# Applying the layer-norm weight vector where tokens are centred instead of in the weights, with weight loads spread over seven units and the next pair's loads gated

## The chip, the cores and the metric

One core of one Trainium2 chip. The metric is device time in microseconds (us) of one execution; lower is better. Every ratio below is to the kernel before, run in turn on the same chip. The runs came from several chips, so a difference of the medians of two runs is rougher than a difference of their ratios.

Engines are named as in the profile: PE is TensorE (matmuls), PEld its weight load, DVE is VectorE, ACT is ScalarE, POOL is GpSimd, SP is SyncE, which here only issues DMAs. The granted clock is the share of full speed that the profile shows for TensorE.

## The reference

Linear attention over 8 batches, 8 heads, 576 positions of 64; then, for each token of 512 numbers, a layer norm, two matmuls with a relu between, and a residual.

```python
def _attn_ref(q, k, v, w_phi):
    def phi(x):
        proj = np.einsum('bhsd,df->bhsf', x, w_phi)
        proj = proj - np.max(np.abs(proj), axis=-1, keepdims=True)
        return np.concatenate([np.exp(proj), np.exp(-proj)], axis=-1)
    ...
    return num / den

def _moe_ref(x, g_ln, w_ch1, w_ch2):
    mu = np.mean(x, axis=-1, keepdims=True)
    var = np.mean((x - mu) ** 2, axis=-1, keepdims=True)
    xn = (x - mu) / np.sqrt(var + 1e-06) * g_ln      # g_ln: 512 numbers
    ch = np.maximum(xn @ w_ch1, 0.0) @ w_ch2         # 512x2048, 2048x512
    return x + ch
```

The vector `g_ln` can be multiplied into the rows of `w_ch1` once (the kernel before) or into every centred token. The division by the standard deviation is done at the very end in both.

## The kernel before

The work is cut into 32 attention units, in four pairs of batches. When a pair's attention is done, its 9 tiles of 128 tokens go through the layer norm and the two matmuls in rounds of three tiles; a round has 16 evictions of the hidden layer (an eviction moves a matmul's result from its tile `hT_ps` to `hT`). While PE multiplies one pair, the other engines prepare the attention of the next. The kernel carries a small list scheduler: every operation is given a cost and a rank, and the kernel is emitted in the order that the scheduler finds. So a change of a cost or of a dependency can reorder all engines.

```python
    def load_w1(n, rank, after):                 # quarter n of w_ch1, 512 KB in bf16, GpSimd's DMA queue
        dma("POOL", rank, 1200000, w1_sb[:, :, n * WC : (n + 1) * WC], ...)

    def scale_w1(n, rank):                       # 4 scalings a chunk, 16 in all
        for kc in range(KC):
            def emit(e, kc=kc):
                w = w1_sb[:, kc, n * WC : (n + 1) * WC]
                ENG[e].tensor_scalar_mul(out=w, in0=w, scalar1=gln_sb[:, kc : kc + 1])
            add_any({"DVE": 0.22, "POOL": 0.62}, rank, emit, r=["gln"], w=[("w1", n, kc)])
    # ... (cut)
            def center(e, i=i, t=t):             # one tile of 128 tokens, on DVE or on POOL
                ENG[e].tensor_scalar(
                    out=pr["xc", r][:, i, :], in0=x[:, t, :],
                    scalar1=pr["mv"][:, t, 0:1], scalar2=None, op0=ALU.subtract,
                )
    # ... (cut)
    WEIGHTS = {0: (0,), 1: (1,), 2: (2,), 3: (3,), 4: (4,), 5: (5,), 6: (6,), 7: (7,)}
    # unit: chunks issued behind its second value scaling (vv); 0 to 3 are w_ch1, 4 to 7 w_ch2
    # ... (cut)
        if n % HG == 1 and 1 <= n < NU - 4:      # q, k, v of a later group of units, then the pair's tails
            g_ = n // HG + 3
            # load_main(...), load_tails(...) on SyncE's queue
```

Of a pair's 576 positions, 512 come as "main" loads (tiles `qk`, `v`, 256 to 512 KB) and the last 64 as "tails" (`qx`, `kx`, `vx`, 64 to 128 KB in short pieces).

## Time and profile before

| | kernel before |
|---|---|
| time, median of 4 runs | 398.87 us (398.62 to 399.58) |
| span of the profiled run | 396.5 us, mean granted clock 0.970 |
| PE busy | 358.1 us, 90% |
| first hT eviction starts | 53.3 us |

First the windows view of the kernel before: busy time of each engine in stretches of the span, then the granted clock and the DMA share.

```profile
core 0: us, PE busy (x) PEld busy (x) DVE busy (x) ACT busy (x) POOL busy (x), PEclk, DMA share, GB/s
0.00:30.00 30.00, 18.67 (x228) 12.21 (x229) 20.48 (x52) 21.14 (x41) 21.75 (x47) 0.97 1.02 258
30.00:60.00 30.00, 20.44 (x241) 14.56 (x241) 27.67 (x71) 23.54 (x50) 26.11 (x44) 0.69 1.04 231
60.00:100.00 40.00, 33.92 (x345) 21.01 (x345) 28.50 (x80) 27.00 (x62) 25.40 (x46) 1.00 0.76 159
100.00:200.00 100.00, 98.46 (x996) 58.30 (x993) 81.02 (x195) 75.17 (x153) 63.51 (x108) 1.00 0.71 173
```

From 100 us on PE is nearly always busy. Before 100 us it lacks 27.0 us (30 − 18.67, 30 − 20.44 and 40 − 33.92), and until 60 us three things are full at once: DMA (share 1.04), VectorE (27.67 of 30) and GpSimd (26.11 of 30). (A share of 1 is all 16 DMA engines busy throughout; the view can come out a little above 1.)

The scalings, and the centrings, in the views of their tiles `w` and `xc` (duration min/median/max in ns; then first and last start in us):

```profile
L363 DVE TENSOR_SCALAR w<-w,gln x11: 341/692/1755, 28.2 to 59.9; 128x512 bf16<-128x512 bf16 x11
L363 POOL TENSOR_SCALAR w<-w,gln x5: 1552/1570/1587, 42.3 to 58.9; 128x512 bf16<-128x512 bf16 x5
...
L853 POOL TENSOR_SCALAR xc<-x,mv x27: 1557/1562/1705, 47.3 to 334.1; 128x512 bf16<-128x512 bf16 x27
...
L853 DVE TENSOR_SCALAR xc<-x,mv x9: 340/346/768, 45.5 to 334.0; 128x512 bf16<-128x512 bf16 x9
```

Sixteen scalings sit in the crowded stretch from 28 to 60 us. The timeline shows three of GpSimd's (4.69 us together) just where PE has its longest gap, 4.72 us:

```profile
42.34 4.69 POOL L363 TENSOR_SCALAR w<-w,gln 128x512 bf16<-128x512 bf16 x3
...
43.85 1.75 DVE L363 TENSOR_SCALAR w<-w,gln 128x512 bf16<-128x512 bf16 x1
...
48.60 0.91 PE L903 MATMUL xT_ps<-ident,xc 128*128 128x128 bf16 x6 [4.72 <-DVE numc L716]
...
48.83 1.04 POOL L615 TENSOR_TENSOR vv<-v,en 128x512 bf16<-128x512 f32 x1
```

GpSimd's next attention work (`vv`) starts at 48.83.

### The profile page before, as it was taken

Reading aid. Unit: us, or ns where it says so; the run is one execution under the profiler, and the core shown is the slowest. Engines: PE = TensorE matmul, PEld = TensorE weight load, DVE = VectorE, ACT = ScalarE, POOL = GpSimd, SP = SyncE. Lnnn points to the kernel's source line nnn. Section 1 sums busy time; section 2 is a strip of 40 time slices with the busy share of each in tenths; the row PEclk is TensorE's granted clock in tenths of the full one; section 3 lists DMA queues with packets and bytes.
Section 4 is the critical chain, followed back from the end, with each engine's and each line's share of the span. In section 5 each row is a group of like instructions: output and inputs, shape, how many; then the busy total and the mean of one; then the engine's idle time right before and its main releaser. Section 6 shows DMA issues by size and latency. Waiting matters only on the chain.

```text
span 396.5 us, 8895 instructions
## 1 busy us (share of the span) xinstructions
PE 358.1 (90%) x3332; PEld 211.0 (53%) x3332; DVE 264.9 (67%) x652; ACT 253.2 (64%) x522; POOL 212.4 (54%) x362
## 2 busy tenths in 40 slices
PE   3858478888999999999999997989999999999994
PEld 2636255544555655555656554655656555555542
DVE  4789899838788977886767988566778676010111
ACT  3888967568698874785878675777766505533310
POOL 4886999636557758676255638744444567000000
PEclk9995689999999999999999999999999999999998
DMA  7999999906587887595445346522210035110102
GB/s 208 312 253 279 179 227 220 269 8 153 170 213 195 228 208 125 137 213 156 109 106 160 78 85 176 104 47 48 55 41 28 29 93 108 27 55 26 49 26 86
DMA packets 88987, 52.42 MB, mean 132 GB/s; under 512 B 55536, under 2 KB 84336, under 8 KB 88944
## 3 DMA queue, kind: packets, MB, share of 16 engines
q1 hardware_dynamic: 83488, 47.07, 47.3%
q0 software_dynamic: 4224, 4.19, 6.7%
q10 hardware_dynamic: 1232, 0.59, 0.6%
q8 instruction: 26, 0.43, 0.5%
q14 instruction: 17, 0.14, 0.1%
HBM read 36.77 MB, written 9.44 MB: 117 GB/s over the span
## 4 chain that ended last, share of the span: by engine, by line
PE 66%; DVE 17%; DMA 8%; issue 3%; ACT 2%; POOL 2%; SPq 0%; DVEq 0%; POOLq 0%; ACTq 0%
PE ch_ps L985 27%; PE hT_ps L953 25%; DVE m L572 5%; PE num L704 3%; PE kv L673 3%; PE pm L553 3%; DMA qkT<-qkb 2%; PE pt L646 2%; DMA kx<-in_k_dram 2%; DVE numc L710 2%; DVE st L847 2%; DVE numc L716 2%; DVE w L363 1%; DMA qk<-in_k_dram 1%; DMA v<-in_v_dram 1%
## 5 line engine op out<-in xcount | busy, mean ns | idle before, releaser
L953 PE MATMUL hT_ps<-xT,w 128*128 128x384 bf16 x768 | 149.5, 326 | 4.3 <-DVE numc L716 1.3
L985 PE MATMUL ch_ps<-w,hT 128*128 128x512 bf16 x576 | 148.4, 379 | 1.7 <-ACT eax L451 0.7
L963 ACT ACTIVATE hT<-hT_ps 128x384 bf16<-128x384 f32 x132 | 64.0, 490 | 73.8 <-PE hT_ps L953 73.5
L953 PEld LDWEIGHTS <-w 128*128 128x128 bf16 x768 | 71.0, 98 | 57.5 <-issue 4.2
L728 POOL TENSOR_TENSOR x<-numc,rden 128x192 bf16<-128x192 f32 (+1 forms) x112 | 50.5, 461 | 67.1 <-DVE rden L722 62.0
L572 DVE TENSOR_REDUCE m<-pm 128x8 f32<-128x1024 f32 x64 | 76.3, 1209 | 12.1 <-PE pm L553 12.1
L985 PEld LDWEIGHTS <-hT 128*128 128x128 bf16 x576 | 52.6, 98 | 47.2 <-DVE numc L716 0.8
L652 ACT ACTIVATE ea<-pt 128x1024 bf16<-128x1024 f32 x64 | 62.2, 1026 | 5.6 <-PE pt L646 5.3
L992 DVE SCALAR_TENSOR_TENSOR o<-ch_ps,rstd,x 128x512 f32<-128x512 f32 x36 | 26.5, 743 | 56.5 <-PE ch_ps L985 43.9
L601 ACT ACTIVATE EB<-pm 128x1024 bf16<-128x1024 f32 x64 | 63.2, 1022 | 1.5 <-DVE m L572 1.5
L615 POOL TENSOR_TENSOR vv<-v,emk 128x512 bf16<-128x512 f32 x32 | 33.5, 1047 | 41.2 <-ACT emk L588 22.5
L853 POOL TENSOR_SCALAR xc<-x,mv 128x512 bf16<-128x512 bf16 x27 | 42.1, 1572 | 8.7 <-DVE mv L848 5.8
L710 DVE TENSOR_TENSOR numc<-num,emq 128x195 f32<-128x195 f32 (+1 forms) x96 | 32.6, 345 | 18.1 <-PE num L704 12.2
L961 DVE TENSOR_SCALAR hT<-hT_ps 128x384 bf16<-128x384 f32 x60 | 32.4, 544 | 13.7 <-PE hT_ps L953 13.2
L704 PEld LDWEIGHTS <-ea 128*128 128x128 bf16 x512 | 28.2, 100 | 18.9 <-issue 3.7
L704 PE MATMUL num<-KV,ea 128*128 128x65 bf16 x512 | 32.5, 197 | 3.9 <-DVE numc L716 1.8
L716 DVE TENSOR_TENSOR numc<-numc,num 128x195 f32<-128x195 f32 (+1 forms) x100 | 33.3, 342 | 1.1
L615 POOL TENSOR_TENSOR vv<-v,en 128x512 bf16<-128x512 f32 x32 | 33.4, 1044 | 0.0
L847 DVE BATCH_NORM_STATS2 st<-x 128x6 f32<-128x512 bf16 x36 | 24.3, 674 | 6.2 <-POOL x L728 6.2
L673 PE MATMUL kv<-vv,EB 128*128 128x65 bf16 x512 | 28.2, 201 | 0.0
L673 PEld LDWEIGHTS <-EB 128*128 128x128 bf16 x512 | 23.9, 103 | 5.3 <-issue 1.6
L553 PEld LDWEIGHTS <-qkT 64*128 64x128 bf16 x512 | 16.0, 100 | 13.1 <-issue 11.0
(67 smaller groups left out, 367.2 us busy)
## 6 DMA issues: line engine op xcount, KB each, us to landing
out_dram<-o SPq DMA_DIRECT2D x32, 256.0 KB, 2.5
qk<-in_k_dram SPq DMA_DIRECT2D x28, 256.0 KB, 3.8
v<-in_v_dram SPq DMA_DIRECT2D x28, 256.0 KB, 3.8
qk<-in_q_dram SPq DMA_DIRECT2D x26, 256.0 KB, 5.1
w<-in_moe_w_ch_dram POOLq DMA_DIRECT2D x8, 512.0 KB, 9.6
qk<-in_k_dram SPq DMA_DIRECT2D x2, 512.0 KB, 8.7
qk<-in_q_dram SPq DMA_DIRECT2D x2, 512.0 KB, 8.4
v<-in_v_dram SPq DMA_DIRECT2D x2, 512.0 KB, 11.4
```

The lines of the kernel that those rows point to most:

```text
L572: nc.vector.reduce_max(out=u["m", i].rearrange("p (c e) -> p e c", e=2), in_=u["pm", i], axis=AX.X, apply_absolute_value=True,)
L601: nc.scalar.activation(u["EB"][:, t].rearrange("p c f -> p (c f)"), u["pm", 1].rearrange("p e c f -> p (e c f)"), AF.Exp, scale=(1.0, -1.0 ...
L615: nc.gpsimd.tensor_tensor(out=u["vv"][:, t, 0:MX, 0:D], in0=vb[:, uu, :].rearrange("p (c d) -> p c d", d=D), in1=bcast(e[:, 0:MX], 2, D), ...
L652: nc.scalar.activation(u["EA"][:, t, :], u["pt"], AF.Exp, scale=(1.0, -1.0)[t])
L673: nc.tensor.matmul(ps[:, t, c // 4, :], EB[:, t, (c % 2) * 4 + c // 2, :], vv[:, t, c, :], start=False, stop=(t == 0 and c == MX - 1), ski ...
L704: nc.tensor.matmul(ps[:, t, i, :], lhsT, rhs, start=(j == 0), stop=(j == len(terms) - 1))
L716: nc.vector.tensor_add(out=st["numc"][:, 0:nch], in0=st["numc"][:, 0:nch], in1=st["ps"][:, 0])
L728: nc.gpsimd.tensor_tensor(out=dst, in0=st["numc"][:, i : i + cnt, 0:D], in1=bcast(st["rden"][:, i : i + cnt], 2, D), op=ALU.mult,)
L853: ENG[e].tensor_scalar(out=pr["xc", r][:, i, :], in0=x[:, t, :], scalar1=pr["mv"][:, t, 0:1], scalar2=None, op0=ALU.subtract,)
L953: nc.tensor.matmul(st["ps"][:, 0:cols], w1_sb[:, kc, jj * P : (jj + 1) * P], pr["xT", r][:, kc, 0:cols], start=(kc == 0), stop=(kc == KC - 1),
L963: nc.scalar.activation(h_sb[:, 0:cols], st["ps"][:, 0:cols], AF.Relu)
L985: nc.tensor.matmul(ch[t], hT[r, jj][:, rt * P : (rt + 1) * P], w2_sb[:, jj, :], start=(jj == 0), stop=(jj == JC - 1),)
```

## The change

The intent: take the 16 scalings out of the crowded stretch by multiplying with `g_ln` while centring; issue the weight chunks earlier; hold pair 1's first loads back behind unit 4 so that pair 0 and the weights have the bandwidth. With it come truer costs for the scheduler, kv products merged into one item, two hidden buffers fewer, and later-emitted centrings. The core of the diff, cut, with explaining comments added:

```diff
-    gln_sb = consts.tile([P, KC], FP32, name="gln")
+    gln_sb = consts.tile([P, DM], FP32, name="gln")        # the vector on every partition, 256 KB
...
-    def scale_w1(n, rank):                                  # the 16 scalings are gone
...
-                ENG[e].tensor_scalar(
-                    out=pr["xc", r][:, i, :], in0=x[:, t, :],
-                    scalar1=pr["mv"][:, t, 0:1], scalar2=None, op0=ALU.subtract,
-                )
+                if e == "DVE":
+                    nc.vector.scalar_tensor_tensor(
+                        out=xc, in0=x[:, t, :], scalar=pr["mv"][:, t, 0:1],
+                        in1=gln_sb, op0=ALU.subtract, op1=ALU.mult,
+                    )
+                else:
+                    xd = moe_sb.tile([P, DM], FP32, tag="xd", name="xd", bufs=1)
+                    nc.gpsimd.tensor_tensor(
+                        out=xd, in0=x[:, t, :], in1=bcast(pr["mv"][:, t, 0], 1, DM),
+                        op=ALU.subtract,
+                    )
+                    nc.gpsimd.tensor_tensor(out=xc, in0=xd, in1=gln_sb, op=ALU.mult)
...
-            add_any({"DVE": 0.25, "POOL": 0.75}, V, center, ...
+            add_any({"DVE": 0.62, "POOL": 2.1}, V, center, ...
...
-    WEIGHTS = {0: (0,), 1: (1,), 2: (2,), 3: (3,), 4: (4,), 5: (5,), 6: (6,), 7: (7,)}
+    GATE = 4
+    WEIGHTS = {0: (0,), 1: (1, 2), 2: (3,), 3: (4,), 4: (5,), 5: (6,), 6: (7,)}
...
+            if n == GATE:                                   # a memset that pair 1's tails must wait for
+                kx1 = kx_bufs[1]
+                add("POOL", 0.1, V, lambda: nc.gpsimd.memset(kx1[:, :, 0:1], 0.0),
+                    r=[("vv", 0, n % 2)], w=[k_ for s_ in range(H) for k_ in tail_keys(1, s_, "k")])
...
+        gs = []
+        if n % HG == 1 and n // HG + 3 != NGRP:
+            gs.append(n // HG + 3)
+        if n == GATE:
+            gs = [NGRP] + gs                                # pair 1's first group comes with unit 4
```

More of the change, by code (lines that the diff above doesn't have):

```diff
@@ L21, in bcast @@
     return dataclasses.replace(ap, ap=new_ap)
-LAG = {"PE": 0.24, "DVE": 0.20, "ACT": 0.23, "POOL": 0.22, "SP": 0.1, "DMA": 1.8}
+LAG = {"PE": 0.24, "DVE": 0.20, "ACT": 0.23, "POOL": 0.22, "SP": 0.1, "DMA": 1.8, "CAST": 1.8}
 class Op:
@@ L127, in run @@
                     for engine in op.alts:
-                        key = op.ready if engine == "DMA" else op.rank
+                        key = op.ready if engine in ("DMA", "CAST") else op.rank
                         heapq.heappush(waiting[engine], (key, op.number, op))
@@ L248, with early @@
     ahead = [E_ATT]
+    E_B, E_A = 0.0, 0.0
+    def early(kw):
+        names = [name for name, _ in kw.get("release") or ()] + [kw.pop("frees", "")]
+        return ahead[0] + (E_B if "B" in names else 0.0) + (E_A if "A" in names else 0.0)
     def add(engine, us, rank, emit, **kw):
+        ahead_of = early(kw)
         sched.add(
-            {engine: us}, rank, (lambda e: emit()) if emit else None, early=ahead[0], **kw
+            {engine: us}, rank, (lambda e: emit()) if emit else None, early=ahead_of, **kw
         )
     def add_any(alts, rank, emit, **kw):
-        sched.add(alts, rank, emit, early=ahead[0], **kw)
+        ahead_of = early(kw)
+        sched.add(alts, rank, emit, early=ahead_of, **kw)
     def mm(n, cols):
@@ L267, in copy_on @@
             ENG[e].tensor_copy(out=dst, in_=src)
-    GBPS = 310.0
     chained = [True]
@@ L279, in dma @@
         chain = ["chain"] if queue == "SP" and chained[0] else []
-        add(queue, {"SP": 0.6, "ACT": 0.4, "POOL": 1.2}[queue], rank, emit, r=r, w=(key, *w, *chain), lag=0.0)
-        add("DMA", nbytes / GBPS / 1000.0, rank, None, r=(key,), w=w)
+        add(queue, {"SP": 0.55, "ACT": 0.55, "POOL": 0.84}[queue], rank, emit, r=r, w=(key, *w, *chain), lag=0.0)
+        if queue == "POOL":
+            add("CAST", 4.8, rank, None, r=(key,), w=w)
+        else:
+            rate = 240.0 if chained[0] else 330.0
+            add("DMA", nbytes / rate / 1000.0, rank, None, r=(key,), w=w)
     def dram(t, offset, ap):
@@ L327, in load_tails @@
             dma(
-                queue, rank, 16384 * len(slots) * 2, dst,
+                queue, rank, 25000 * len(slots), dst,
                 dram(t, off + 512 * D, [[D, 64], [step, len(slots)], [1, D]]),
@@ L356, in load_w1 @@
         )
-    @early_weights
-    def scale_w1(n, rank):
-        for kc in range(KC):
-            def emit(e, kc=kc):
-                w = w1_sb[:, kc, n * WC : (n + 1) * WC]
-                ENG[e].tensor_scalar_mul(out=w, in0=w, scalar1=gln_sb[:, kc : kc + 1])
-            add_any({"DVE": 0.22, "POOL": 0.62}, rank, emit, r=["gln"], w=[("w1", n, kc)])
     @early_weights
@@ L509, in turn @@
                 )
-            add_any({"POOL": 1.1, "ACT": 0.95, "DVE": 0.6}, V, cast,
+            add_any({"POOL": 1.0, "ACT": 0.95, "DVE": 0.8}, V, cast,
                     r=main_keys(u, "k") + main_keys(u, "q"), w=[("qkb", n % 2)])
             ks = [("qkT", i, n % NQ) for i in range(2)]
-            add("SP", 0.7, V, turn, r=[("qkb", n % 2)], w=[("turn", n), *ks], lag=0.0)
+            add("SP", 1.27, V, turn, r=[("qkb", n % 2)], w=[("turn", n), *ks], lag=0.0)
             add("DMA", 1.0, V, None, r=[("turn", n), ("qkb", n % 2)], w=ks)
@@ L631, in a_side @@
             add("ACT", 0.91, V, lambda t=t: exps(t), r=[ps_key, ("m", 1, n % 3)],
-                w=[("EB", t, n % 2)], release=[("A", 1)] if t else None)
+                w=[("EB", t, n % 2)], release=[("A", 1)] if t else None, frees="A")
         vdata = [*main_keys(u, "v"), *tail_keys(u["pair"], u["slot"], "v")]
@@ L657, in a_feat @@
             add("ACT", 0.91, V, lambda t=t: exps(t), r=[("pt", n)], w=[("EA", t, n % 2)],
-                release=[("A", 1)] if t else None)
+                release=[("A", 1)] if t else None, frees="A")
     def a_kv(u, V):
@@ L680, in copy @@
             nc.scalar.copy(out=u["KV"], in_=u["kv"])
-        us = mm(1, 130) + mm(MX, 70)
-        add("PE", us, V, lambda: products(1),
-            r=[("EB", 1, n % 2), ("EBx", g % 2), ("vv", 1, n % 2)], w=[("kv", n)],
-            acquire=("B", 1))
-        add("PE", us, V, lambda: products(0),
-            r=[("EB", 0, n % 2), ("EBx", g % 2), ("vv", 0, n % 2)], w=[("kv", n)])
+        us = 2 * (mm(1, 130) + mm(MX, 70))
+        add("PE", us, V, lambda: (products(1), products(0)),
+            r=[(what, t, n % 2) for what in ("EB", "vv") for t in range(2)] + [("EBx", g % 2)],
+            w=[("kv", n)], acquire=("B", 1))
         add("ACT", 0.27, V, copy, r=[("kv", n)], w=[("KV", n % NKV)], release=[("B", 1)])
@@ L852, in center @@
                     pr["xc", r] = moe_sb.tile([P, NM, DM], BF16, tag="xc", name="xc")
-                ENG[e].tensor_scalar(
-                    out=pr["xc", r][:, i, :], in0=x[:, t, :],
-                    scalar1=pr["mv"][:, t, 0:1], scalar2=None, op0=ALU.subtract,
-                )
+                xc = pr["xc", r][:, i, :]
+                if e == "DVE":
[3 more added lines that the diff above has]
+                    )
+                else:
+                    xd = moe_sb.tile([P, DM], FP32, tag="xd", name="xd", bufs=1)
[4 more added lines that the diff above has]
+                    nc.gpsimd.tensor_tensor(out=xc, in0=xd, in1=gln_sb, op=ALU.mult)
             w = [("mv", pair % 2, t)]
@@ L861, in x_stats @@
             add("DVE", 0.72, V, stats, r=[("x", pair % NX, t, h) for h in range(H)], w=w)
-            add_any({"DVE": 0.25, "POOL": 0.75}, V, center, r=[("mv", pair % 2, t)] + [("x", pair % NX, t, h) for h in range(H)],
+            add_any({"DVE": 0.62, "POOL": 2.1}, V, center, r=["gln"] + [("mv", pair % 2, t)] + [("x", pair % NX, t, h) for h in range(H)],
                     w=[("xc", slot, i)])
@@ L869, in rstd @@
             nc.scalar.activation(pr["rstd"][:, sl], pr["rstd"][:, sl], AF.Exp, scale=-0.5)
-        add("ACT", 0.35, V + 3.0, rstd, r=[("mv", pair % 2, t) for t in ts],
+        add("ACT", 0.44, V + 3.0, rstd, r=[("mv", pair % 2, t) for t in ts],
             w=[("rstd", pair % 2, t) for t in ts])
@@ L892, in x_trans @@
                 key, wk = ("xturn", pr["pair"], r, i), [("xT", slot, 0, i), ("xT", slot, 2, i)]
-                add("SP", 0.7, V, turn, r=[("xc", slot_c, i)], w=[key, *wk], lag=0.0)
+                add("SP", 1.27, V, turn, r=[("xc", slot_c, i)], w=[key, *wk], lag=0.0)
                 add("DMA", 0.5, V, None, r=[key, ("xc", slot_c, i)], w=wk)
@@ L938, in store @@
                 )
-    HB = 2 * JC + 2
+    HB = 2 * JC
     def moe(pr, V):
@@ L999, in second @@
                 r=[("rstd", pair % 2, t)] + [hkey[r, jj] for jj in js]
-                + [("w2", jj) for jj in js],
+                + [("w2", jj) for jj in (js if j0 or pair else range(JC))],
                 w=[("ch", pair, t)], acquire=("B", 1) if j0 == 0 else None)
@@ L1007, in second @@
                 key = ("store", pair, t)
-                add("SP", 0.6 if t < MX else 1.2, 0.0, lambda: store(pr, t, ch["o", t]),
+                add("SP", 0.42 if t < MX else 1.2, 0.0, lambda: store(pr, t, ch["o", t]),
                     r=[ok], w=[key], lag=0.0)
@@ L1014, in moe @@
             m = len(tiles[r - 1]) if r else 0
+            if r < NR and ("slot", r) not in pr:
+                ahead[0] = E_X
+                v_ = pr["V"] + 3 * r
+                x_trans(pr, r, x_stats(pr, r, v_), v_)
             for jj in range(JC):
                 if r < NR:
-                    ahead[0] = E_M0 if r + pair == 0 else E_MOE
+                    ahead[0] = E_M0 if pair == 0 and r < TILES0 else E_MOE
                     first(r, jj, V)
@@ L1024, in moe @@
                         n = min(end - i, JC - i % JC)
-                        ahead[0] = E_S0 if r == 1 and pair == 0 else E_MOE
+                        ahead[0] = E_S0 if pair == 0 and r <= TILES0 else E_MOE
                         second(r - 1, i, n, V)
@@ L1063 @@
     load_tails(v, 0, [0], "SP", 0.4)
-    dma("ACT", 0.5, 2048, gln_sb, moe_g_ln.rearrange("(kc p) -> p kc", p=P), w=["gln"])
+    dma("ACT", 0.5, 262144, gln_sb, dram(moe_g_ln, 0, [[0, P], [1, DM]]), w=["gln"])
     load_main(k, 0, [1], "SP", 0.6)
@@ L1126 @@
                     load_w1(i_, V, after)
-                    scale_w1(i_, V)
                 else:
@@ L1154 @@
             if i == H - 1:
-                for r in range(TILES0 if w_["pair"] == 0 else 0, len(pr["tiles"])):
-                    v_ = V + 0.9 * step + 3 * r
-                    x_trans(pr, r, x_stats(pr, r, v_), v_)
+                pr["V"] = V + 0.9 * step
                 ahead[0] = E_MOE
@@ L1160 @@
             ahead[0] = E_ATT
-        if n % HG == 1 and 1 <= n < NU - 4:
-            g_ = n // HG + 3
+        gs = []
[3 more added lines that the diff above has]
+            gs = [NGRP] + gs
+        for g_ in gs:
             if g_ < NG:
-                for i_, t_ in enumerate((k, q, v)):
-                    load_main(t_, g_, [0, 1], "SP", V + 0.1 * i_)
                 if g_ % NGRP == 0:
                     for i_, t_ in enumerate((k, q, v)):
-                        load_tails(t_, g_ // NGRP, None, "SP", V + 0.05 + 0.1 * i_)
-            if n == 5:
+                        load_tails(t_, g_ // NGRP, None, "SP", V + 0.1 * i_)
+                for i_, t_ in enumerate((k, q, v)):
+                    load_main(t_, g_, [0, 1], "SP", V + 0.5 + 0.1 * i_)
+            if g_ == NGRP + 1:
                 chained[0] = False
```

## The prediction

> **What bounds it now.** From about 60 us on, TensorE: in the windows view PE is busy 285.1 of the 292 us from 100 to 392; then a 5 us tail (last eviction, store). A gain must come from the first 100 us, where PE is idle 27 us, 3.6 of them before the first data. From 27 to 52 us the granted clock is 0.59, which inflates the 16.9 us of PE work there by roughly 5 us (estimate). What holds PE up is first DMA (the chain waits 8.9 us for the k tails, 12 to 21 us), then VectorE (8.9 to 9.6 us busy of each 10 from 20 to 70), with GpSimd behind it (up to 9.8).
>
> **Removed.** 16 weight scalings between 28 and 62 us (lines view): 11 on VectorE, 8.9 us (0.34 us at best, up to 1.75), 5 on GpSimd, 7.8 us. About 5.8 us of the VectorE ones lie on the chain, and three on GpSimd (4.7 us at 42.3) delay unit 5's value scaling until 48.8. There PE has its longest wait: 4.7 us before the xT transposes at 48.6.
>
> **Added.** Centring becomes a two-tensor op. On VectorE I estimate 0.65 to 0.7 us, against 0.34: the o eviction, of the same form and size, took 0.74 from PSUM; the Trainium skill, "VectorE: DVE Perf Modes", section "The perf-mode tier table", has fp32 tensor_tensor at 1x and tensor_scalar in faster modes, which the 0.34 us suits. On GpSimd two tensor_tensors of about 1.04 each (as the vv scaling), 2.1 against 1.56. Over 36 tiles about +14 us of GpSimd or +3 of VectorE, nearly all after 65 us, where neither bounds. A few tenths show in pair 0's rounds 1 and 2, whose centring is on the chain at 79 to 82 us. The weight vector's load grows from 2 to 256 KB in the busiest DMA stretch: about 1 us at 250 to 310 GB/s (estimate).
>
> **Moved.** Weight chunks 2 to 7 are issued one unit earlier: chunk 7, now issued at 66.4 us and landing at about 76, should land before 60, so second matmuls can start well before 74. Pair 1's first group and tails (35 to 60 us now) wait for unit 4's vv, about 40 us, leaving bandwidth to pair 0 and weights; they should still land by about 60, before unit 8 needs them. Merged kv products, 32 hidden buffers for 34 and the deferred centring: under 1 us each. The scheduler's truer durations may trim DMA-transpose waits on the chain (2.4%, 9 us), but PE's idle time after 100 us is only 7 us.
>
> **Sum.** Earlier end of pair 0's attention and first MoE matmul (51.7 us now, about 44 then): 6 to 9 us. Warmer clock and second matmuls in the gaps from 50 to 100: 3 to 5. After 100: 0 to 3. Against: gln broadcast and dearer centring, 1 to 2. Net about 11.5: 387 us, range 379 to 395. Chances: faster by over 2% 0.72, within 2% 0.26, slower 0.02.
>
> **What would show it.** No scaling lines; first hT matmul at 43 to 46 us; first ch_ps before 65; no 4.7 us PE gap; PE idle in 0 to 100 about 16 us; clock above 0.59 in 27 to 52; PE about 92% of the span; xc on VectorE near 0.7, on GpSimd two ops near 1.05.
>
> **What would make it wrong.** The new order fills the freed slots with other work; pair 1's gated loads arrive late and PE idles at 65 to 90 us; or DMA, not VectorE, limits pair 0 from 20 to 50 us.

## The result, and the profile after

Ratios here and below are the mean time of one kernel's fast runs over the mean of the other's fast runs of the same rounds, so they are not quite the ratios of the medians quoted.

| | before | after |
|---|---|---|
| median of 4 runs | 398.87 us (398.62 to 399.58) | 402.53 us (401.48 to 402.78) |
| ratio, 95% interval | 1 | 1.0084 (1.0061 to 1.0107) |
| span and clock of the profiled run | 396.5 us, 0.970 | 400.9 us, 0.982 |
| first hT eviction starts | 53.3 us | 55.1 us |
| first round of hT done | 74.3 us | 79.7 us |
| second, third, fourth round done | 111.9, 145.3, 171.8 | 114.5, 151.0, 176.3 |
| last round done, last output computed | 383.7, 392.3 | 387.8, 396.4 |

The new kernel is right, and 0.84% slower, and outside the predicted range of 379 to 395 us. A round is done when its last eviction ends. The lag of about 5 us is there by 80 us, shrinks to 2.6 in the second round, is 5.7 after the third and settles at about 4 us.

The windows of the kernel after, same stretches:

```profile
core 0: us, PE busy (x) PEld busy (x) DVE busy (x) ACT busy (x) POOL busy (x), PEclk, DMA share, GB/s
0.00:30.00 30.00, 17.31 (x233) 12.49 (x236) 21.05 (x57) 21.94 (x44) 22.84 (x50) 1.00 1.01 248
30.00:60.00 30.00, 17.70 (x228) 12.77 (x232) 21.27 (x57) 19.29 (x40) 22.69 (x43) 0.77 1.04 210
60.00:100.00 40.00, 32.17 (x358) 20.30 (x360) 35.34 (x90) 30.68 (x67) 28.55 (x51) 1.00 1.01 245
100.00:200.00 100.00, 94.10 (x924) 55.88 (x934) 79.66 (x188) 67.05 (x139) 57.50 (x99) 1.00 0.66 150
```

VectorE and GpSimd were relieved from 30 to 60 us (27.67 to 21.27 us, 26.11 to 22.69 us), yet PE did less there, not more. Its deficit before 100 us grew from 27.0 to 32.8 us. DMA stayed full. (49 matmul records are missing from this trace, 40 of them of the second matmul, so PE's idle time is somewhat overstated; the table of finished rounds does not depend on them.) The clock did rise from 0.69 to 0.77, with less work to run at it.

The centrings in the tile views of the kernel after; the two GpSimd lines are the two steps of one centring:

```profile
L861 POOL TENSOR_TENSOR xd<-x,mv x19: 1040/1041/1390, 45.3 to 334.1; 128x512 f32<-128x512 bf16 x19
L865 POOL TENSOR_TENSOR xc<-xd,gln x19: 1262/1271/1800, 46.5 to 335.2; 128x512 bf16<-128x512 f32 x19
```

```profile
L855 DVE SCALAR_TENSOR_TENSOR xc<-x,mv,gln x17: 719/1307/1828, 47.7 to 336.9; 128x512 bf16<-128x512 bf16 x17
```

No scaling line is left. Alone, VectorE's centring costs what was estimated (0.72 us), but its median is 1.31 us.

PE's longest waits in the first 100 us of the kernel before, in the waits view (total, times, longest):

```profile
PE qkT_ps L523 <- DMA qk<-in_k_dram: 5.2, 3, 3.6
PE xT_ps L903 <- DVE numc L716: 5.1, 2, 4.7
```

and in the kernel after:

```profile
PE xT_ps L394 <- issue: 6.8, 1, 6.8
PE pt L648 <- DVE m L574: 5.5, 4, 1.7
PE qkT_ps L525 <- DMA qk<-in_k_dram: 4.7, 2, 3.8
```

The 4.7 us gap at 44 us is gone, and a gap of 6.75 us at 28.7 us has come. The profile calls its cause "issue", because it sees no semaphore. What PE is about to do there says more; the timeline of the kernel after:

```profile
35.46 0.37 PE L394 MATMUL xT_ps<-ident,qx 128*128 128x128 bf16 x2 [6.75 <-issue]
```

It transposes `qx`, pair 0's q tails. Their two loads, issued at 18.4 and 19.2 us, land at 32.9 and 35.4 us; in the kernel before, issued at 17.1 and 18.7, they land at 28.5 and 29.2. What stands in their way is shown by the DMA view of 25 to 30 us. Queue q1 carries SyncE's loads and q0 the weights that GpSimd issues. Before:

```profile
q1 hardware_dynamic: 1517, 1.09, 81.4%
q0 software_dynamic: 296, 0.29, 34.3%
```

After:

```profile
q0 software_dynamic: 777, 0.77, 91.3%
q1 hardware_dynamic: 712, 0.26, 30.0%
```

The columns are packets, MB and share of time. With three weight chunks issued between 13.7 and 20.1 us (before: two) the weights take nearly three times the bytes in this stretch, and the loads that pair 0 waits for a quarter of theirs. The Trainium skill, "DMA: Bandwidth & Descriptors", section "Queues, rings and completion order", says that each DMA engine goes round-robin between its queues one packet at a time. The trace agrees: 777 packets against 712, and from 26 to 28 us alone 319 against 320. But a weight packet has 0.99 KB (0.77 MB / 777) and one of the queue with the tails 0.37 KB, so equal turns are far from equal bytes. Pair 0's last group of k, q and v landed at 30.5, 32.8 and 37.0 us before, and at 39.3, 42.9 and 45.2 us after.

Pair 1 was held back by more than the gate. SyncE issues in a fixed order, and the scheduler had put loads of later groups and of pair 2 ahead of pair 1's first group. In the waits view for SyncE from 25 to 70 us of the kernel after:

```profile
SPq L284 <- PE kv L675: 12.6, 2, 12.1
```

SyncE's queue stood still from 31.9 to 43.4 us, and pair 1's first six main loads landed at 61.4 to 65.9 us instead of 39.6 to 45.3.

So there were two suspects for the loss. **Theory D**: early weights and a late, reordered SyncE queue starve pair 0 and pair 1 of data. **Theory C**: the dearer centring costs more than was thought. A third, **theory G**, blames the gate alone. Rival to all: the scheduler's new order of everything.

### The profile page after: what moved, and what is told of

The parts are those of the page before. It is cut to its first block, busy times and chain, and to the rows that moved or that the text cites. A ratio compares the mean times of both kernels' runs of the same rounds, so it can differ in the third digit from the quotient of the medians.

```text
span 400.9 us, 8845 instructions
## 1 busy us (share of the span) xinstructions
PE 351.3 (88%) x3283; PEld 208.7 (52%) x3332; DVE 278.4 (69%) x658; ACT 246.1 (61%) x511; POOL 210.8 (53%) x371
## 5 line engine op out<-in xcount | busy, mean ns | idle before, releaser
L994 PE MATMUL ch_ps<-w,hT 128*128 128x512 bf16 x536 | 141.2, 379 | 4.4 <-DVE numc L716 1.4
L972 ACT ACTIVATE hT<-hT_ps 128x384 bf16<-128x384 f32 x126 | 61.7, 492 | 74.4 <-PE hT_ps L962 73.8
L654 ACT ACTIVATE ea<-pt 128x1024 bf16<-128x1024 f32 x64 | 63.2, 1039 | 8.2 <-PE pt L648 6.8
L603 ACT ACTIVATE EB<-pm 128x1024 bf16<-128x1024 f32 x64 | 64.1, 1028 | 2.4 <-DVE m L574 2.4
L710 DVE TENSOR_TENSOR numc<-num,emq 128x195 f32<-128x195 f32 (+1 forms) x96 | 32.9, 347 | 22.0 <-PE num L704 17.3
L970 DVE TENSOR_SCALAR hT<-hT_ps 128x384 bf16<-128x384 f32 x66 | 35.5, 542 | 8.2 <-PE hT_ps L962 7.2
L704 PEld LDWEIGHTS <-ea 128*128 128x128 bf16 x512 | 28.6, 99 | 18.7 <-issue 3.0
L861 POOL TENSOR_TENSOR xd<-x,mv 128x512 f32<-128x512 bf16 x19 | 20.8, 1094 | 11.1 <-DVE mv L848 10.0
L865 POOL TENSOR_TENSOR xc<-xd,gln 128x512 bf16<-128x512 f32 x19 | 25.3, 1331 | 1.5
L648 PE MATMUL pt<-qkT,wbk 128*128 128x512 bf16 x55 | 18.0, 397 | 8.0 <-DVE m L574 6.5
L675 PE MATMUL kv<-vv,EB 128*128 128x65 bf16 x512 | 24.8, 199 | 0.0
```

The source lines that it names most:

```text
L603: nc.scalar.activation(u["EB"][:, t].rearrange("p c f -> p (c f)"), u["pm", 1].rearrange("p e c f -> p (e c f)"), AF.Exp, scale=(1.0, -1.0 ...
L654: nc.scalar.activation(u["EA"][:, t, :], u["pt"], AF.Exp, scale=(1.0, -1.0)[t])
L704: nc.tensor.matmul(ps[:, t, i, :], lhsT, rhs, start=(j == 0), stop=(j == len(terms) - 1))
L710: nc.vector.tensor_tensor(out=st["numc"][:, 0:nch], in0=st["ps"][:, 1], in1=bcast(em_of(), 2, D1), op=ALU.mult,)
L970: nc.vector.tensor_relu(h_sb[:, 0:cols], st["ps"][:, 0:cols])
L972: nc.scalar.activation(h_sb[:, 0:cols], st["ps"][:, 0:cols], AF.Relu)
```

## The experiments

Where "order kept" is said, the scheduler made its list from the unchanged source and only the named edit was applied to that list, so that nothing else moved. Otherwise the scheduler ordered anew. All were timed in 5 rounds. Five results are wrong, as said at each. The medians are over all runs of a kernel, the ratios over the fast ones alone; only e9 (one run) and e10 (two) had slow runs, and their fast runs alone have medians of 396.89 and 397.94 us. An interval is about ±0.2 to 0.5%, or 1 to 2 us.

| run | median us | before, same chip | ratio (95% interval) |
|---|---|---|---|
| e1 after, weights late | 402.15 | 398.68 | 1.0076 (1.0043 to 1.0110) |
| e2 before, weights early | 403.74 | 398.68 | 1.0117 (1.0075 to 1.0159) |
| e3 after, one chunk a unit, reordered | 404.66 | 398.68 | 1.0146 (1.0112 to 1.0180) |
| e4 before, centring with weight | 397.84 | 398.68 | 0.9987 (0.9955 to 1.0019) |
| e5 after, weights late, SyncE order | 401.37 | 398.80 | 1.0067 (1.0029 to 1.0105) |
| e6 after, SyncE order | 401.31 | 398.80 | 1.0058 (1.0020 to 1.0095) |
| e7 before, no scalings (wrong) | 394.72 | 398.80 | 0.9890 (0.9843 to 0.9938) |
| e8 after, cheap centring (wrong) | 397.36 | 398.80 | 0.9953 (0.9916 to 0.9990) |
| e9 after, GpSimd's centrings cheap (wrong) | 397.89 | 398.89 | 0.9961 (0.9914 to 1.0009) |
| e10 after, VectorE's centrings cheap (wrong) | 398.16 | 398.89 | 0.9975 (0.9930 to 1.0019) |
| e11 = e4, all centrings on VectorE | 400.55 | 398.89 | 1.0016 (0.9967 to 1.0065) |
| e12 before, all scalings on VectorE | 398.78 | 398.89 | 1.0000 (0.9952 to 1.0047) |
| e13 = e8 and e5 together (wrong) | 397.24 | 399.73 | 0.9920 (0.9890 to 0.9951) |
| e14 after, no gate, reordered | 401.90 | 399.73 | 1.0067 (1.0045 to 1.0089) |
| e15 before, scalings moved later | 399.72 | 399.73 | 1.0008 (0.9970 to 1.0045) |

### e1 and e2: the time of the weight loads alone

```diff
  # the emission order is kept; only the weight DMAs are moved in it
- chunk -> unit  {0: 0, 1: 1, 2: 1, 3: 2, 4: 3, 5: 4, 6: 5, 7: 6}
+ chunk -> unit  {0: 0, 1: 1, 2: 2, 3: 3, 4: 4, 5: 5, 6: 6, 7: 7}    # e1, in the kernel after
# e2 is the same edit the other way round, in the kernel before
```

> The kernel after, with every engine's instruction order kept and only the eight weight DMAs moved in the GpSimd queue: chunk c right after unit c's second value scaling, as in the kernel before (after has chunks 1 and 2 at unit 1 and every later one a unit earlier). Theory D (the early chunks starve pair 0's own loads): q tails land by about 30 us instead of 35.4, group 2's q by about 35 instead of 42.9, the 6.75 us PE gap at 28.7 us falls under 2 us, and the time falls from 402.5 to 395 to 398 us. Rivals: S (the new order itself, from the new durations, is slower), G (pair 1's gated loads), C (dearer centring): PE gap stays within 1 us of 6.75 or, if it closes, the time stays at 401 to 404 us.

> The kernel before, order kept, only the weight DMAs moved to where after has them (chunks 1 and 2 at unit 1, later ones a unit earlier). D: q tails land at 33 to 36 us instead of 29.2 and PE, which wants them at 30.8, waits 3 us or more; group 2 lands 4 us or more later than 30.5 to 37.0; time rises from 398.9 to 401 to 405 us. S, G, C: nothing of theirs is in it, so 398 to 399.5, or a little less because the weights come earlier.

Measured: e2 confirmed that early weights do harm in the kernel before, 1.17% or 4.7 us. In its waits view PE now waits for the same tails, and the profile names them:

```profile
PE xT_ps L410 <- DMA qx<-in_q_dram: 4.3, 1, 4.3
```

But e1 gained nothing to speak of. Its first gap did shrink, from 6.75 to 1.09 us, and the first hT eviction came at 48.3 us; then a new gap of 6.6 us opened at 59.5 us:

```profile
PE num L723 <- ACT KV L701: 6.7, 2, 6.6
...
DVE qkb L291 <- DMA qk<-in_q_dram: 7.9, 1, 7.9
```

VectorE, whose list has a fixed order, does nothing for 7.9 us (56.5 to 64.4) before a cast of pair 1's q, which lands only at 62.2 to 64.3 us; everything behind that cast waits, PE included. So restoring pair 0's loads turned one wait into another. Theory D alone, in its first form, fell.

### e3: the same spread by way of the source

```diff
- WEIGHTS = {0: (0,), 1: (1, 2), 2: (3,), 3: (4,), 4: (5,), 5: (6,), 6: (7,)}
+ WEIGHTS = {0: (0,), 1: (1,), 2: (2,), 3: (3,), 4: (4,), 5: (5,), 6: (6,), 7: (7,)}
```

> The kernel after with the old spread of one weight chunk per unit over eight units in its source, so that the scheduler orders everything anew. D: 393 to 398 us, no PE gap over 3 us between 20 and 45 us. S, G or C: 400 to 404 us.

A miss: 404.66 us. The scheduler made another order, with an 8.1 us wait of PE at 70.3 us for a DMA transpose of `qkT`. It says little about the weights and much about the method: a source edit in this kernel moves everything, and that is why most later runs keep the order.

### e4: the centring alone

```diff
# in the kernel before: the new center(), its costs and its dependence on gln,
# gln on every partition, no call of scale_w1, HB = 2 * JC
```

> The kernel before with the part that names the change alone: weight vector at the centring, 256 KB broadcast load, no weight scaling, and 32 hidden buffers instead of 34 because the vector and the scratch tile need the memory. If removing the scalings is worth what the prediction said (6 to 9 us less 1 to 2), 391 to 395 us and a first hT matmul at 44 to 47 us. C (dearer centring eats it): 398 to 402 us. If VectorE was not what held pair 0 up: 396 to 399 us.

397.84 us, 0.13% below before and not to be told from it. PE's deficit before 100 us fell from 27.0 to 23.8 us and the second round ended 6.6 us earlier (105.3 against 111.9 us); from 140 to 180 us PE then idles more than before, with gaps of 2.9 and 1.6 us (this trace, too, lacks 48 matmul records, about 5 of them in that stretch), and the fifth round ends at 198.6 us against 199.3. The lead is given back. Moving the vector without the rest of the change is therefore free of harm, but worth nothing here.

### e5 and e6: SyncE's order

```diff
# order kept; in SyncE's list pair 2's k and q tails and group 6's k and q loads
# go behind pair 1's second group.  e6: in the kernel after; e5: in e1
```

> e1 (after with the old weight times) and, in the SP queue only, pair 2's k and q tails and group 6's k and q loads moved from in front of pair 1's first group to behind group 5; every compute order kept. Theory H, added to D: in e1 the head of the SP queue waited for PE's last k-tail transposes of pair 0 (27.9 to 35.9 us) and pair 1's first q landed only at 62.2 to 64.3, where VectorE's cast of unit 8 blocked 7.9 us and PE 6.55. D and H: pair 1's first group lands before 56 us, that gap closes, first hT round ends by 75 instead of 80.7, time 394 to 398 us. If the new order itself (S) or the centring (C) is the loss: 400 to 403 us.

> After with the SP queue of e5 but its own early weights. D and H: the first gap (6.75 us at 28.7, q tails starved by weights) stays, the second limit goes; since after reached that second limit 0.4 us late only, the time gains 1 to 3 us: 399.5 to 402 us. If the queue's order alone were the cause: 395 to 398 us.

401.37 and 401.31 us: both about 1 us better than the kernel after, less than an interval. For e5, 394 to 398 us had been expected: a miss. In e5 the wait at 59.5 us of e1 is gone, and a wait of 3.4 us for a DMA transpose at 69.4 us is new; in e6, which came out inside its expected 399.5 to 402 us, the first gap of 5.5 us for the tails stays. The queue is real, but it is not most of the loss.

### e7 and e8: what the scalings are worth, and what the centring costs

```diff
# e7: kernel before, order kept, the scalings not emitted (the vector is then left out: wrong)
-                ENG[e].tensor_scalar_mul(out=w, in0=w, scalar1=gln_sb[:, kc : kc + 1])
+                return
# e8: kernel after, order kept, the old one-input centring (the vector is left out: wrong)
+                ENG[e].tensor_scalar(out=xc, in0=x[:, t, :], scalar1=pr["mv"][:, t, 0:1],
+                                     scalar2=None, op0=ALU.subtract)
```

> Before with its order kept and the 16 weight scalings not emitted (wrong result on purpose: the layer norm weight is left out). The pure worth of the removed work. The prediction's reading (VectorE holds pair 0 up): 391 to 395 us and the 4.7 us PE gap at 43.9 gone. If the loads hold it up: 396 to 399 us.

> After with its order kept and the old centring (one tensor_scalar, no weight; wrong result on purpose). C (dearer centring takes the gain): 396 to 399 us. D and H: 400.5 to 402.5 us, the two early limits unchanged.

These two gave the frame of the explanation. Leaving the scalings out is worth 4.1 us (398.80 − 394.72), not the 6 to 9 predicted, though the time is still within the 391 to 395 us expected for the prediction's reading; the gap of 4.7 us shrinks to 2.1 (it begins at 43.9 us as before) and does not vanish:

```profile
PE xT_ps L903 <- DVE numc L716: 2.5, 2, 2.1
```

And with the cheap centring the kernel after is 5.2 us faster (402.53 − 397.36; by the ratios 1.31 points, also 5.2 us), and then even ahead of before. VectorE's centrings are then short:

```profile
L854 DVE TENSOR_SCALAR xc<-x,mv x17: 321/348/973, 47.2 to 328.6; 128x512 bf16<-128x512 bf16 x17
```

What the dear centring costs does not come where pair 0 starts (e8 has the early lag too), but by steps at the centrings of the later pairs:

| hT rounds done, us | 1st | 2nd | 3rd | 4th | 5th | 7th | 8th | 10th | 12th |
|---|---|---|---|---|---|---|---|---|---|
| before | 74.3 | 111.9 | 145.3 | 171.8 | 199.3 | 261.8 | 288.4 | 340.2 | 383.7 |
| after | 79.7 | 114.5 | 151.0 | 176.3 | 204.1 | 265.0 | 291.4 | 344.3 | 387.8 |
| e8 | 80.5 | 113.6 | 149.0 | 172.4 | 200.1 | 260.0 | 286.4 | 337.5 | 381.0 |

From after to e8 the difference is −0.8 us in the wrong direction at the first round, 2.0 at the third, 3.9 at the fourth, 5.0 at the seventh and 6.8 at the last. Theory C stands. (Over all, e8's profiled run is 6.8 us ahead and the medians 5.2.)

### e9 and e10: why the centring is dear

Two rivals: one engine's part costs and the other's doesn't, or the two only cost together. In each run one engine's centrings are one-input again (the diffs are shortened).

```diff
# e9: only GpSimd's centrings (wrong on those tiles)
-                    nc.gpsimd.tensor_tensor(out=xd, ...); nc.gpsimd.tensor_tensor(out=xc, in0=xd, in1=gln_sb, ...)
+                    nc.gpsimd.tensor_scalar(out=xc, in0=x[:, t, :], scalar1=mean, op0=ALU.subtract)
# e10: only VectorE's centrings (wrong on those tiles)
-                    nc.vector.scalar_tensor_tensor(out=xc, in0=x[:, t, :], scalar=mean, in1=gln_sb, ...)
+                    nc.vector.tensor_scalar(out=xc, in0=x[:, t, :], scalar1=mean, op0=ALU.subtract)
```

> After, order kept, with GpSimd's 19 centrings as one tensor_scalar each (one tensor input; wrong result on purpose, those tiles get no weight); VectorE's 17 stay two-input. Theory X: VectorE's two-input op and GpSimd's two-input op cannot run together, whoever comes second waits, so in after VectorE's op took 0.72 us alone and up to 1.83 beside GpSimd. X expects VectorE's mean to fall from 1.22 to under 0.85 us and 3 to 5 of e8's 5 us to be recovered: 397.5 to 399.5 us. If the cost were VectorE's own slower form: VectorE's mean stays over 1.1 us and 401 to 402.5 us.

> The reverse of e9: VectorE's 17 centrings are the old tensor_scalar, GpSimd's 19 stay two two-input ops each (wrong result on purpose). X: VectorE's op still waits behind GpSimd's in places (0.34 us alone, mean 0.5 to 0.9), 400 to 401.5 us. If VectorE's own slower form is the cost: mean 0.4 us and 397.5 to 399.5 us.

The times, 397.89 and 398.16 us, are those of e8 (397.36) within the noise: either half alone takes back most of the 5 us. For e10 400 to 401.5 us had been expected, so that was a miss: the two halves do not add. For e9 this is clear. For e10 it is less sure: its two runs set aside as slow (403.27 and 404.52 us) were so called for their time, while their clocks (0.964 and 0.968) are like those of its fast runs (0.963 to 0.983); with them its mean would be 399.6 us, and about half of the 5 us taken back. Both profiles fell in the slow state (e9's span is 532 us at a clock of 0.657, e10's 401.5 at 0.964), so only durations of single VectorE and GpSimd ops are read from them. The centrings on VectorE, in e9:

```profile
L855 DVE SCALAR_TENSOR_TENSOR xc<-x,mv,gln x17: 719/745/2394, 49.1 to 434.7; 128x512 bf16<-128x512 bf16 x17
```

and in e10, where the op is the one that took 0.35 us before:

```profile
L855 DVE TENSOR_SCALAR xc<-x,mv x17: 321/860/1708, 47.9 to 336.6; 128x512 bf16<-128x512 bf16 x17
```

Sorting VectorE's centrings by what GpSimd was already doing when they started, with at least 0.3 us of it to go, gives:

| VectorE's centring | beside GpSimd's one-input op | beside GpSimd's two-input op |
|---|---|---|
| one-input (before, e7, e8; e10) | 0.34 to 0.35 us in 7 of 8 cases, 0.77 in one | 0.45 to 1.36 us, median 1.17 (e10, 8 cases) |
| two-input (e9; after) | 0.74 us (e9, 3 cases) | 1.25 to 1.75 us, median 1.57 (after, 8 cases) |

At these centrings it is GpSimd's two-input op that stops VectorE: in all 16 cases of the right-hand column VectorE's op ended 0.15 us (one-input) or 0.55 us (two-input) after GpSimd's. The timeline of the kernel before shows a one-input op inside another without harm:

```profile
74.54 1.56 POOL L853 TENSOR_SCALAR xc<-x,mv 128x512 bf16<-128x512 bf16 x1 [1.12 <-DVE mv L848]
...
75.25 0.34 DVE L853 TENSOR_SCALAR xc<-x,mv 128x512 bf16<-128x512 bf16 x1
```

But that is a matter of the moment, and GpSimd's one-input op stops VectorE too. The scalings are the same pair of ops, and in the same profile three of VectorE's, which take 1.02 us if each takes 0.34, took 1.61 (0.74, 0.34 and 0.69):

```profile
58.89 1.56 POOL L363 TENSOR_SCALAR w<-w,gln 128x512 bf16<-128x512 bf16 x1
58.99 1.61 DVE L363 TENSOR_SCALAR w<-w,gln 128x512 bf16<-128x512 bf16 x3
```

The scaling of 1.75 us shown at the start ended 0.15 us after the second of GpSimd's three. In the traces of all runs together, 26 of VectorE's one-input ops on such a tile (centrings and scalings) started inside a GpSimd one-input op with at least 0.3 us of it to go. The 12 that started 0.57 to 0.79 us into it, and 3 that started together with it, took 0.34 to 0.35 us; the 8 that started 0.09 to 0.42 us into it took 0.43 to 0.77, and the 3 that started 0.84 to 1.02 us into it took 0.69 to 0.88 and ended 0.15 us after it. So the 7 of 8 in the table owe much to when those centrings happened to start.

The kernel after, at pair 1's centrings:

```profile
149.69 1.26 POOL L865 TENSOR_TENSOR xc<-xd,gln 128x512 bf16<-128x512 f32 x1
...
149.93 2.23 DVE L855 SCALAR_TENSOR_TENSOR xc<-x,mv,gln 128x512 bf16<-128x512 bf16 x2
...
152.08 0.35 DVE L710 TENSOR_TENSOR numc<-num,emq 128x195 f32<-128x195 f32 x1
```

The two centrings of the second line took 1.57 and 0.74 us: the first began 0.25 us after GpSimd's op and ended 0.55 us after its end, the second ran alone. The other way round it is GpSimd that waits: at 47.96 us its `xd` took 1.39 us, not 1.04, because VectorE's centring had started at 47.73. The Trainium skill states this: "SBUF — State Buffer", section "Who interferes with whom", says that a VectorE instruction with two inputs in SBUF contends with a GpSimd instruction that reads SBUF, and that whichever comes first holds the port while the other waits. This case agrees for two-input against two-input ops. Whether the e9 cell of the table disagrees hangs on one case; see the last section.

What this comes to on VectorE, summed over all its centrings in each profile:

| | before | e8 | e10 | e9 | after |
|---|---|---|---|---|---|
| VectorE's centrings, count and sum | 9, 4.1 us | 17, 6.6 us | 17, 13.7 us | 17, 14.5 us | 17, 20.7 us |
| median time of the kernel | 398.87 us | 397.36 us | 398.16 us | 397.89 us | 402.53 us |

Of the 14.1 us between e8 and after, some 6 are the longer op itself (17 × (0.72 − 0.35)) and some 8 the blocking. Both half steps take 6 to 7 us off VectorE and get 4.6 (e9) and 4.4 us (e10, with the reserve above) of time; the other 7 to 8 us get nothing that can be measured. GpSimd's own longer work does not explain the loss: its centrings sum to 46.1 us in the kernel after and still to 44.3 in e10 (30.7 in e9). The reading that fits is that VectorE has slack in these bursts for about 14 us of centring and not for 20.7. It is a reading: blocking as such, without the longer op, was not tried, and e10 keeps part of the blocking with most of the loss gone. That the blocking happens, and that it makes up the larger part of VectorE's added time, is shown.

The cost is not peculiar to the new order. e4, with the new centring in the order of before, and e7, with neither centring nor scalings, differ by 0.97 points (0.9987 − 0.9890), or 3.9 us; but e4 was reordered.

### e11 and e12: would one engine alone be better?

```diff
# e11: e4 with            e12: the kernel before with
- add_any({"DVE": 0.62, "POOL": 2.1}, V, center    - add_any({"DVE": 0.22, "POOL": 0.62}, rank, emit
+ add_any({"DVE": 0.72}, V, center                 + add_any({"DVE": 0.5}, rank, emit
```

> e4 (before with the centring change alone, 397.84 us) with all 36 centrings on VectorE, a right result. X: every one takes about 0.72 to 0.9 us, GpSimd is freed of some 45 us, and the time falls to 394 to 396.5 us, below before. If VectorE's added work (about 26 us in all) is what counts: 397.5 to 400 us.

> Before with the 16 weight scalings kept and all put on VectorE, a right result. e7 says the scalings cost about 4 us in all; the five on GpSimd took 1.57 us each where the scheduler believed 0.62, and three of them held up unit 5. If most of the 4 us is GpSimd's: 395.5 to 397.5 us. If it is VectorE's: 398 to 400 us.

No. In e11, with the order made anew, GpSimd has no centrings left and the contention is nearly gone (two of 36 still took 1.00 and 1.09 us, beside other GpSimd ops),

```profile
L855 DVE SCALAR_TENSOR_TENSOR xc<-x,mv,gln x36: 718/743/1086, 44.0 to 337.4; 128x512 bf16<-128x512 bf16 x36
```

but VectorE then has 36 centrings to do itself, and the time is 400.55 us, not to be told from before. e12 is equal to before: taking the scalings off GpSimd opens no way either, at least in the order that the scheduler then made.

### e13, e14 and e15: does it add up, is it the gate, and is there a better version

```diff
# e13: kernel after, order kept: e8's centring, e1's weight times, e5's SyncE order
# e14: kernel after, reordered: no memset, and
- GATE = 4
+ GATE = 3
# e15: kernel before, reordered: pair 0 takes the vector where its transposes leave PSUM,
#      and VectorE scales w1 in place between pair 0's rounds and pair 1's
-                copy_on(e, pr["xT", r][:, k0 : k0 + 2, 0:cols], ...)
+                for kk in range(2):  # a copy with a scale for each partition, on ACT or DVE
+                    nc.scalar.mul(dst, src, g_)   # or nc.vector.tensor_scalar_mul(...)
```

> Wrong on purpose: the kernel after with its order kept, with the cheap centring of the kernel before (no weight vector), its weight chunks issued at the old times (chunk c after unit c), and pair 2's tails and group 6's loads put behind pair 1's first groups in SyncE's list. It takes both suspected losses out at once. If the loss is the sum of dearer centring (-5.2 us when it was undone alone) and of early loads and a queue order (-0.4 to -1.2 us when undone alone, +4.7 us when put into the kernel before), this must come to the level of the kernel before without its scalings: 394 to 396.5 us, ratio 0.988 to 0.994. If what is left is the new order of all engines itself, it stays where the cheap centring alone left it: 397 to 398.5 us, ratio 0.995 to 1.0.

> The kernel after without its gate on the next pair's first loads (result right; the scheduler orders the rest anew). If the gate is what turned SyncE's list round and cost the lead, pair 1's first loads land before 50 us again, and the time falls to 398 to 400 us. If the dear centring and the early weight loads are the cost and the gate is not, it stays at 400.5 to 404 us.

> A candidate, result right: the kernel before with its cheap centring, in which pair 0 takes the weight vector where its transposes are copied out of PSUM (two copies of 384 columns with a scale for each partition in place of one of 768), and VectorE scales w1 in place between pair 0's and pair 1's rounds. If the worth of the scalings is only that they stand in the way of the first hT evictions, this keeps most of the 4.1 us that leaving them out gave: 395 to 397.5 us, ratio 0.99 to 0.997. If the 16 VectorE scalings cost as much in the later place, it is 398 to 400 us.

e13 came to a ratio of 0.992, in the expected band of 0.988 to 0.994. Its 397.24 us lies in the rival's band of 397 to 398.5, but before itself ran at 399.73 us on that chip, a microsecond slower than on the others, so the ratio decides. Its interval (0.9890 to 0.9951) overlaps that of e7 and also that of e8 (0.9916 to 0.9990). So with both losses taken out the new order is about as good as the old one without its scalings, a separate cost of the order itself could not be shown, and what e1 and e5 add on top of e8 is too small to be established. One wait of 7.8 us is still in it, at 64 us, again for a DMA transpose:

```profile
PE pm L580 <- DMA qkT<-qkb: 7.8, 1, 7.8
```

e14 removed the gate: pair 1's first six main loads landed at 51.3 to 55.0 us, ten us sooner, and the time stayed at 401.90 us (ratio 1.0067 against 1.0084, less than an interval apart), with the first gap (6.7 us, for the tails) unchanged. Theory G fell, though in an order made anew.

e15, the candidate, is right and equal to before (1.0008). It was ahead by 7.1 us after the first round (67.2 us) and by 10.4 after the second (101.5), and lost that by the fourth (172.3 against 171.8). In its windows view PE idles 7.1 us from 130 to 180 us, where before idled 1.1:

```profile
130.00:180.00 50.00, 42.93 (x373) 24.45 (x370) 37.42 (x94) 31.85 (x65) 32.19 (x46) 0.97 0.67 151
```

No other engine is full there. It looks as though PE had run out of prepared work, as in e4: both led early and gave it back in the same stretch. No right version was found that beats the kernel before.

## Why the prediction was wrong, point by point

The result, read as shares of before's time on each chip: leaving out the scalings is worth −1.10 points (e7), the dearer centring costs 1.31 (after 0.84, e8 −0.47). The early weights and the queue cost a further 0.33 (e8 −0.47, e13 −0.80), and 0.30 remain (e13 −0.80, e7 −1.10). These add to 0.84 by construction; with intervals of 0.3 to 0.5 points only the first two terms are established one by one.

- **"Net about 11.5: 387 us": wrong.** 402.53 us. Three terms of the sum failed.
- **"Earlier end of pair 0's attention and first MoE matmul (51.7 us now, about 44 then): 6 to 9 us": the step that failed first.** The durations of the scalings were taken as time on the critical path. With the order kept and the scalings gone (e7) the first hT eviction came only 3.0 us earlier (50.3 against 53.3), and the run ended 4.1 us earlier. In the whole change the first eviction was 1.8 us later, not earlier.
- **"Against: gln broadcast and dearer centring, 1 to 2", "nearly all after 65 us, where neither bounds": the second failed step, and the larger.** The stand-alone durations were right (0.72 us measured, 0.65 to 0.7 estimated; `xd` 1.04), and wrong as a cost: beside GpSimd's two-input op VectorE's took 1.25 to 1.83 us. (GpSimd's second op took 1.27, not 1.05.) The cost is 5.2 us (e8), and it falls in the later pairs, where the prediction saw none. That VectorE's average share of the span is 67% did not mean that it had time to spare in the bursts at the centrings.
- **"Warmer clock and second matmuls in the gaps from 50 to 100: 3 to 5": did not come.** The clock did rise (0.69 to 0.77 from 30 to 60 us) and chunk 7 landed at 69.3 us instead of 75.0, not before 60. But the first second matmul ran at 81.0 us (74.0 before), where "before 65" had been predicted, and PE idled 32.8 us of the first 100 instead of 16. Issuing the weights early delayed pair 0's q tails by 4 to 6 us (issued late, in e1, they landed at 29.1 and 29.7 us, as before). In the kernel before the same edit cost 4.7 us (e2); in the kernel after its undoing gave 0.4 us, less than an interval (e1).
- **"They should still land by about 60": wrong by little.** Pair 1's first loads landed at 61.4 to 65.9 us. It mattered less than thought: ten us sooner changed nothing (e14).
- **"No 4.7 us PE gap", "no scaling lines", "on GpSimd two ops": right; "xc on VectorE near 0.7": only alone** (median 1.31 us). And the gap was not owed to the scalings alone: 2.1 us of it stayed in e7.
- **"Or DMA, not VectorE, limits pair 0 from 20 to 50 us"**, under what would make it wrong: this came true in the kernel after, whose longest gap in the first 100 us (6.75 us) is for pair 0's q tails. The share of DMA was 1.04 before the change: relieving VectorE in a stretch where DMA is full need not buy what VectorE's durations suggest (e7: 4.1 us), and the sum of the prediction did not allow for it.
- The perf-mode table that the prediction took from the Trainium skill ("VectorE: DVE Perf Modes", "The perf-mode tier table") fits what was measured of an op alone: the one-input op took 0.34 us, the two-input one with an fp32 vector 0.72. What two inputs do next to GpSimd, which the page on SBUF says, is not in the prediction's sum.

What stays open: how much of the loss is early weights, how much SyncE's order and how much mere order. In the kernel before early weights cost 4.7 us (e2); in the kernel after undoing them gave 0.4 us (e1), undoing the queue order 1.2 us (e6), both 1.2 us (e5), each below an interval. And why the leads of e4 and e15 are lost at 130 to 180 us was seen and not tested.

## What to carry to other kernels

An op's duration alone is not its price: an op of VectorE and one of GpSimd can wait for each other, here in all 16 tabled cases in which GpSimd's had two inputs, and the cost is to be counted in the burst in which both run, not against an average share. When several resources are full in a stretch, the relief of one can be worth less than its durations say (here 4.1 us for 16.7 us of scalings), so measure that first by leaving the work out with the order kept, wrong result and all. And in a kernel whose order is found by a scheduler, test a change at a fixed order, since each edit of the source otherwise tests another order.

## What the Trainium skill lacked or had wrong

- "SBUF — State Buffer", "Who interferes with whom": a two-input VectorE op is said to contend with any GpSimd instruction that reads SBUF. In e9 three such ops started inside GpSimd's one-input op (1.56 us, which reads SBUF) and took 0.74 us, as alone. Two of them started 0.71 and 0.78 us into it, where one-input ops ran free as well; only the third, 1.07 us into it, speaks against the page. A GpSimd one-input op that came second did stretch, from 1.56 to 1.97 us, as the page says. All this is from a profile; a targeted run was not made.
- The same section: whichever op comes first is said to hold the shared ports for its whole instruction. Against GpSimd's two-input op that fits (e10: all 8 ended 0.15 us after it). GpSimd's one-input op of 1.56 us did not hold them throughout: VectorE's one-input op took 0.34 to 0.35 us in all 12 cases in which it started 0.57 to 0.79 us into it, and 0.43 to 0.88 in the 11 in which it started earlier (from 0.09 us on) or later (to 1.02).
- "GPSIMD Engine Reference": there is a duration for a two-input op, but none for a one-input one. Here the one-input subtraction of 128x512 bf16 took 1.56 us and the two-input one of the same tile, written as fp32, 1.04 us.
- "VectorE: DVE Perf Modes", "The perf-mode tier table": no row for the op with a scalar and two tensors. Here 128x512 bf16 with an fp32 vector took 0.72 us alone.
- "DMA: Bandwidth & Descriptors", "Queues, rings and completion order": the rule of packet turns is there, but not what follows from it for loads in short pieces. Here 777 packets of 0.99 KB against 712 of 0.37 KB left the short ones a quarter of the bytes (0.26 of 1.03 MB). The page counts several descriptors to a packet; whether the packets that the profile counts are the same was not shown.
